# Loading the first two pairs with two neighbouring tokens per partition, and issuing the weights after the second and fourth batch

## The chip, the cores and the metric

The kernel runs on one NeuronCore of a Trainium2 chip. The metric is the device time of one execution in microseconds (us). Besides the timed runs there is one profiled execution, with a trace of every instruction. Five engines work side by side: TensorE (PE; its weight loads are shown as PEld), VectorE (DVE), ScalarE (ACT), GpSimd (POOL) and SyncE (SP), which issues transfers. Each engine executes its own instructions in the order in which they were written; semaphores make one engine wait for another.

## What is computed

A gated linear attention over four batches of eight heads, 768 tokens and a head dimension of 48, and after it a feed-forward layer over all 3072 tokens:

```
f = 1 / (1 + exp(-f_logit))
for t in range(S):
    state = f[:, :, t, :, None] * state + einsum('bhd,bhe->bhde', k[:, :, t], v[:, :, t])
    y[:, :, t] = einsum('bhd,bhde->bhe', q[:, :, t], state)
x = y as (batch * tokens, 384)
h = x @ w_in            # 384 -> 2048
g = maximum(0.01 * h, h)
out = g @ w_out         # 2048 -> 384
```

Inputs and outputs are float32 in the chip's main memory.

## The kernel before

The recurrence is cut into chunks of 128 tokens, six per batch. A *pair* j is one chunk of two batches, so there are twelve pairs, two for each chunk; pairs 0 and 1 hold the first chunk of batches 0, 1 and 2, 3. In the names below the first number is the pair, the second the batch of the pair (0 or 1; a 2 stands for both), the third a part. The steps of a pair are these:

- `Lf`, `Lk`, `Lq`, `Lv` (`load`, line 96): SP loads one input of one batch, 192 KB, with a token on each of 128 partitions. A partition gets eight separate runs of 192 bytes, one per head. `inp` has six buffers per input.
- `gate` (118) on ScalarE: exp and ln give the log of the gate, `lf`. The two instructions take 128x384 elements for one batch; from pair 4 on both batches at once.
- `cs` (124) on TensorE: a matmul with the upper triangle `ut` sums `lf` over the tokens, and four small ones with `ones_col` sum it over the whole chunk. `dec` (133) on ScalarE takes the exponentials of these.
- `k` and `q` (143, 149): k and q are scaled. `K_DVE` and `Q_DVE` say for how many pairs that is done on VectorE; after that it is done on POOL.
- `v` (155) on POOL: two casts of v, `v_b` and `v2`.
- `tk`, `tq` (170) transpose on TensorE, `ck`, `cq` (175) copy the result out on VectorE.
- `sc` (184): the scores q·k, 16 matmuls for both batches. `mk` (195): VectorE multiplies them with the triangle. `mx` (201): 32 matmuls of 32 columns each for two batches (56 where there is a state from earlier chunks), which give `py`; `xt` (229) copies that into `xT`.
- `pt`, `sf`, `sb` (233, 239, 244): the state of the chunk on TensorE, its addition on VectorE, its decay and cast on POOL.
- `up` (251): six matmuls with `w_in`, eight such groups in a pair; `pr` (260): the leaky relu on ScalarE; `dn` (264): four matmuls with `w_out`, eight such groups in a pair; `ob` (270) on VectorE and `st` (274) on SP: the copy and the store of 128 rows of the result.
- `WI` and `WO` (`weights`, 101): POOL copies one element of a loaded input into `gate_w`, and by that waits for this load; then it issues the transfers of `w_in` (nine) or `w_out` (four), which cast to bfloat16 on the way.

All of this is written in one long list of words, `order` (292 to 348), and emitted in that order; no scheduler moves anything. So an engine's order of work is the order of its words in the list: what is behind a waiting instruction on the same engine waits as well. The tag `g` of the PSUM has four buffers, used in turn by `cs`, `tp`, `pw`, `py` and `pt`; `pm` and `po` have two each.

Before the list come the constants (59 to 83): on VectorE the zeroing of the padding columns, on POOL `ut`, `ident`, `ones_col`, then `v2s` and the states.

In the list before, SP loads in the order f, f, k, q, v of pair 0 and then the rest in turn; `WI_1` stands behind `q_1_1` and waits for the second v load of pair 1, `WO_2` waits for that of pair 2. On POOL `v_0_0`, `v_0_1` and `v_1_0` stand ahead of `WI_1`, `v_1_1` behind it.

Of the kernel before, what the change touches and what calls it, by code (L numbers as in the profile page):

```python
# [9 lines left out]
FP32 = mybir.dt.float32  # L10
# [5 lines left out]
def kernel(  # L16
# [23 lines left out]
    BY_UNIT = 4  # L40
    K_DVE = 3
    Q_DVE = 2
# [31 lines left out]
    nc.gpsimd.memset(ones_col, 1.0)  # L74
    gate_w = const.tile([1, 8], FP32, tag="gate_w")
# [20 lines left out]
    def load(j, name, a):  # L96
        c, h = pairs[j]
        nc.sync.dma_start(out=raw(j, name)[:, a],  # L98
                          in_=srcs[name][2 * h + a, :, c * C:(c + 1) * C, :].rearrange("h t d -> t h d"))

    def weights(which, j):

        nc.gpsimd.tensor_copy(out=gate_w[:, 0:1], in_=raw(j, "v")[0:1, 1, H - 1, D - 1:D])
        if which == "in":
            for lo, hi in ((0, FF // 4), (FF // 4, FF // 2), (FF // 2, FF)):
                for kk in range(NK):
                    nc.gpsimd.dma_start(out=w_in_b[:, kk, lo:hi], in_=moe_w_in[kk * 128:(kk + 1) * 128, lo:hi])
        else:
            n = NF // 4
            for part in range(4):  # L110
                nc.gpsimd.dma_start(  # L111
                    out=w_out_b[:, part * n:(part + 1) * n, :],
                    in_=moe_w_out[part * n * 128:(part + 1) * n * 128, :].rearrange("(a p) n -> p a n", p=128))
# [3 lines left out]

    def gate(j, i):
        e = work.tile([128, 2, H, D], FP32, name="e_t", tag="e_t")
        a = half(j, i)  # L120
        nc.scalar.activation(e[:, a], raw(j, "f")[:, a], AF.Exp, scale=-1.0)  # L121
        nc.scalar.activation(lfs[j % NR][:, a, :, 0:D], e[:, a], AF.Ln, bias=1.0)  # L122

    def cs(j, a):
        lf = lfs[j % NR]
        t = st[j]["cs", a] = ps_g.tile([128, 512], FP32, name="cs", tag="g")
        nc.tensor.matmul(t[:, 0:H * D], ut, lf[:, a, :, 0:D], start=True, stop=True)  # L127
# [5 lines left out]
    def dec(j, a):  # L133
# [5 lines left out]
        if pairs[j][0] < NCH - 1:  # L139
# [3 lines left out]
    def scale_k(j, i):  # L143
        a = half(j, i)
        eng = nc.vector if j < K_DVE else nc.gpsimd
        eng.tensor_mul(khs[j % NR][:, a, :, 0:D], raw(j, "k")[:, a],  # L146
                       st[j]["em"][:, a].rearrange("t a (h d) -> t a h d", d=D))

    def scale_q(j, i):
        a = half(j, i)  # L150
        eng = nc.vector if j < Q_DVE else nc.gpsimd
        eng.tensor_mul(qhs[j % NR][:, a, :, 0:D], raw(j, "q")[:, a],  # L152
                       st[j]["a"][:, a].rearrange("t a (h d) -> t a h d", d=D))

    def cast_v(j, i):
# [3 lines left out]
        nc.gpsimd.tensor_copy(out=vb[:, a], in_=raw(j, "v")[:, a])  # L159
        nc.gpsimd.tensor_copy(out=v2[:, P2 * a.start:P2 * a.stop, 0:4:3, :],  # L160
                              in_=raw(j, "v")[:, a].rearrange("t a (p j) d -> t (a p) (j d)", j=2)[:, :, 32:64]
# [13 lines left out]
    def turn_out(j, a, x):  # L175
        nc.vector.tensor_copy(out=turned(j, x)[:, P2 * a:P2 * a + P2, :], in_=st[j].pop(("tp" + x, a)))  # L176
# [4 lines left out]
    def units(a):  # L181
        return range(2) if a == 2 else (a,)

    def score(j, a2):
        kT, qT = st[j]["kT"], st[j]["qT"]
        for a in units(a2):
            for i in range(2):
                st[j]["pw", a, i] = ps_g.tile([128, P2, 128], FP32, name="pw", tag="g")
            for p in range(P2):
# [5 lines left out]
    def mask(j, a, i):  # L195
        wm = st[j]["wm", a, i] = work.tile([128, P2, 128], BF16, name="wm", tag="wm", bufs=8)
        nc.vector.tensor_mul(wm, st[j].pop(("pw", a, i)), ut[:, None, :].to_broadcast([128, P2, 128]))  # L197
# [3 lines left out]
    def mix(j, a2):  # L201
# [10 lines left out]
        for a in units(a2):  # L212
# [16 lines left out]
    def x_out(j, a):  # L229
        xT = once(j, "xT", lambda: work.tile([128, NK, 2, 128], BF16, name="xT", tag="xT", bufs=3))  # L230
        nc.vector.tensor_copy(out=xT[:, :, a, :], in_=st[j].pop(("py", a))[:, 0:NK, :])  # L231

    def state(j, a):
        pt = st[j]["pt", a] = ps_g.tile([128, P2, 2 * D], FP32, name="pt", tag="g")
# [39 lines left out]
    def store(j, a):  # L274
# [13 lines left out]
        "WI": lambda j: weights("in", j), "WO": lambda j: weights("out", j),  # L288
# [4 lines left out]
    Lf_0_0 Lf_0_1 Lk_0_0 Lq_0_0 Lv_0_0 gate_0_0 Lf_1_0 gate_0_1 cs_0_0 Lk_0_1 dec_0_0 cs_0_1 Lq_0_1 dec_0_1 k_0_0  # L293
    Lv_0_1 v_0_0 q_0_0 tk_0_0 Lf_1_1 tq_0_0 ck_0_0 gate_1_0 pt_0_0 Lk_1_0 cq_0_0 sf_0_0 sc_0_0 Lq_1_0 cs_1_0 k_0_1
    q_0_1 Lv_1_0 tk_0_1 dec_1_0 v_0_1 mk_0_0_0 Lf_2_0 mk_0_0_1 tq_0_1 gate_1_1 Lk_1_1 ck_0_1 mx_0_0 cq_0_1 pt_0_1
    k_1_0 Lq_1_1 sb_0_0 sc_0_1 xt_0_0 Lv_1_1 mk_0_1_0 cs_1_1 v_1_0 mk_0_1_1 Lf_2_1 dec_1_1 sf_0_1 Lk_2_0 gate_2_0
    q_1_0 mx_0_1 tk_1_0 Lq_2_0 sb_0_1 xt_0_1 tq_1_0 pt_1_0 k_1_1 cs_2_0 Lv_2_0 dec_2_0 q_1_1 WI_1 ck_1_0 cq_1_0 tk_1_1
    gate_2_1 sf_1_0 tq_1_1 ck_1_1 sc_1_0 cq_1_1 cs_2_1 mk_1_0_0 dec_2_1 mk_1_0_1 sc_1_1 up_0_0 mk_1_1_0 v_1_1 mx_1_0
    mk_1_1_1 pr_0_0 up_0_1 Lf_3_0 sb_1_0 xt_1_0 mx_1_1 pr_0_1 pt_1_1 xt_1_1 up_0_2 sf_1_1 up_1_0 pr_0_2 k_2_0 sb_1_1
    pr_1_0 up_0_3 tk_2_0 pr_0_3 up_1_1 ck_2_0 pr_1_1 up_1_2 Lk_2_1 pr_1_2 up_1_3 Lq_2_1 up_0_4 q_2_0 pr_1_3 Lv_2_1  # L300
    pr_0_4 up_0_5 v_2_0 Lf_3_1 tq_2_0 pr_0_5 up_0_6 cq_2_0 gate_3_0 Lk_3_0 pt_2_0 up_1_4 sf_2_0 Lq_3_0 pr_0_6 cs_3_0
    k_2_1 q_2_1 pr_1_4 up_0_7 Lv_3_0 dec_3_0 tk_2_1 WO_2 tq_2_1 ck_2_1 up_1_5 cq_2_1 pr_0_7 sc_2_2 pr_1_5 up_1_6
    gate_3_1 mk_2_0_0 mk_2_0_1 up_1_7 pr_1_6 v_2_1 mk_2_1_0 cs_3_1 pr_1_7 mk_2_1_1 pt_2_1 dec_3_1 dn_0_0_0 sf_2_1
    mx_2_2 Lf_4_0 dn_1_0_0 xt_2_0 sb_2_0 xt_2_1 dn_0_0_1 sb_2_1 dn_1_0_1 up_2_0 k_3_0 pr_2_0 up_2_1 dn_0_0_2 pr_2_1
    dn_1_0_2 tk_3_0 up_2_2 Lk_3_1 ck_3_0 pr_2_2 up_2_3 Lq_3_1 dn_0_0_3 q_3_0 pr_2_3 Lv_3_1 dn_1_0_3 ob_0_0 v_3_0
    tq_3_0 Lf_4_1 ob_1_0 dn_0_1_0 cq_3_0 dn_1_1_0 st_0_0 dn_0_1_1 k_3_1 st_1_0 dn_1_1_1 q_3_1 dn_0_1_2 Lk_4_0 dn_1_1_2
    v_3_1 Lq_4_0 Lv_4_0 dn_0_1_3 gate_4_0 dn_1_1_3 ob_0_1 Lf_5_0 tk_3_1 ob_1_1 tq_3_1 up_2_4 st_0_1 ck_3_1 pt_3_0
    cq_3_1 pt_3_1 pr_2_4 up_2_5 st_1_1 sf_3_0 dn_2_0_0 sf_3_1 pr_2_5 Lk_4_1 up_2_6 Lq_4_1 sc_3_2 Lv_4_1 pr_2_6 up_2_7
    mk_3_0_0 Lf_5_1 dn_2_0_1 mk_3_0_1 pr_2_7 cs_4_0 Lk_5_0 mk_3_1_0 dn_2_0_2 dec_4_0 mk_3_1_1 cs_4_1 Lq_5_0 dn_2_0_3
    dec_4_1 mx_3_2 ob_2_0 Lv_5_0 v_4_0 dn_2_1_0 xt_3_0 st_2_0 xt_3_1 gate_5_0 dn_2_1_1 sb_3_0 Lf_6_0 up_3_0 Lk_5_1  # L310
    dn_2_1_2 sb_3_1 pr_3_0 Lq_5_1 up_3_1 k_4_0 dn_2_1_3 Lv_5_1 pr_3_1 up_3_2 ob_2_1 Lf_6_1 dn_3_0_0 pr_3_2 q_4_0
    tk_4_0 st_2_1 tk_4_1 ck_4_0 up_3_3 ck_4_1 Lk_6_0 pt_4_0 pt_4_1 pr_3_3 tq_4_0 sf_4_0 tq_4_1 up_3_4 Lq_6_0 cq_4_0
    v_5_0 Lv_6_0 dn_3_0_1 cq_4_1 pr_3_4 sf_4_1 up_3_5 gate_6_0 Lf_7_0 sc_4_2 up_3_6 Lk_6_1 mk_4_0_0 pr_3_5 mk_4_0_1
    Lq_6_1 cs_5_0 pr_3_6 up_3_7 mk_4_1_0 Lv_6_1 dec_5_0 dn_3_0_2 mk_4_1_1 cs_5_1 Lf_7_1 cs_6_0 pr_3_7 mx_4_2 dec_5_1
    Lk_7_0 dn_3_0_3 xt_4_0 sb_4_0 dec_6_0 Lq_7_0 cs_6_1 xt_4_1 dn_3_1_0 ob_3_0 sb_4_1 dec_6_1 Lv_7_0 up_4_0 dn_3_1_1
    st_3_0 pr_4_0 k_5_0 up_4_1 gate_7_0 Lf_8_0 dn_3_1_2 up_4_2 q_5_0 Lk_7_1 pr_4_1 dn_3_1_3 Lq_7_1 pr_4_2 tk_5_0
# [65 lines left out]
```

## Time and profile before

| | us |
|---|---|
| median of 3 runs | 198.18 |
| lowest and highest run | 196.0, 198.26 |
| the profiled execution | 197.44 |
| its span in the trace | 195.7 |
| TensorE busy | 177.3 (91%) |
| ScalarE, VectorE, POOL busy | 98.4, 93.4, 83.3 |
| bytes moved, mean rate | 27.08 MB, 138 GB/s |

The profiled execution is 1.74 us longer than its span; the median is 0.74 us above that execution. The profile's page gives the busy time of each engine, and the same in 40 slices of 4.9 us, a digit being tenths of a slice. The timeline shows start, duration, engine and line of instructions, and in brackets the idle time before them and what ended it. In a line of the table of stretches each engine has its busy time in that stretch, then come the granted TensorE clock, the mean share of the 16 DMA engines that was busy, and GB/s.

### The profile page before, as it was taken

To read this page: it belongs to the slowest core of one execution; us is meant where nothing else is said; L and a number is where in the kernel's file an instruction comes from. 1 tells how busy PE (TensorE), PEld (TensorE's weight loads), DVE (VectorE), ACT (ScalarE), POOL (GpSimd) and SP (SyncE) were. 2 spreads that over 40 slices of the span, in tenths; PEclk is the share of its full clock that TensorE was granted. 3 is DMA by queue.
4 is the path that set the end of the run, shared out by engine and by line. 5 is a ranking of instruction groups with operands and counts; after the bars stand their busy time and mean duration, and the time that the engine had idled before them with its cause. 6 is when DMAs were issued, how large, how long until landed. Compare 5 with 4: busy or idle time off the path is not lost.

```text
span 195.7 us, 5241 instructions
## 1 busy us (share of the span) xinstructions
PE 177.3 (91%) x2152; PEld 130.7 (67%) x2152; DVE 93.4 (48%) x203; ACT 98.4 (50%) x197; POOL 83.3 (43%) x145
## 2 busy tenths in 40 slices
PE   0686379999999999999979999999999999999993
PEld 0455237777667687787756867777777777777761
DVE  2699614273327438347581149168373146553111
ACT  5645415893234748776155752854324736154430
POOL 8145845928400762795332902984204420500000
PEclk9999999999999999999996999999999999999999
DMA  6999999899999999899999999220001110110112
GB/s 134 216 216 185 166 196 208 162 183 186 190 222 215 222 198 226 159 228 219 200 201 232 183 232 209 44 78 6 18 27 40 45 40 3 40 40 3 40 44 80
DMA packets 106728, 27.08 MB, mean 138 GB/s; under 512 B 100432, under 2 KB 106320, under 8 KB 106704
## 3 DMA queue, kind: packets, MB, share of 16 engines
q1 hardware_dynamic: 103296, 23.60, 57.1%
q0 software_dynamic: 3408, 3.15, 10.1%
q8 instruction: 17, 0.28, 0.6%
q14 instruction: 7, 0.06, 0.1%
HBM read 25.17 MB, written 4.72 MB: 153 GB/s over the span
## 4 chain that ended last, share of the span: by engine, by line
PE 69%; DMA 15%; SPq 11%; POOL 2%; issue 1%; ACT 1%; DVE 1%; POOLq 0%
PE po L267 30%; PE pm L256 25%; SPq L98 10%; DMA q_raw<-in_q_dram 7%; DMA w_out_b<-in_moe_w_out_dram 7%; PE py L225 4%; PE tp L173 4%; PE pw L192 2%; DMA f_raw<-in_f_logit_dram 1%; PE cs L127 1%; POOL w_out_b L111 1%; PE pt L236 1%; SPq L277 1%; POOL qh L152 0%; ACT e_t L121 0%
## 5 line engine op out<-in xcount | busy, mean ns | idle before, releaser
L262 ACT ACTIVATE gT<-pm 128x512 bf16<-128x512 f32 x96 | 57.0, 598 | 75.0 <-PE pm L256 74.5
L256 PE MATMUL pm<-xT,w_in_b 128*128 128x256 bf16 x576 | 79.7, 278 | 5.0 <-DMA w_in_b<-in_moe_w_in_dram 3.6
L267 PE MATMUL po<-w_out_b,gT 128*128 128x384 bf16 x384 | 75.9, 328 | 0.1
L256 PEld LDWEIGHTS <-w_in_b 128*128 128x128 bf16 x576 | 54.8, 99 | 19.1 <-DMA w_in_b<-in_moe_w_in_dram 4.4
L267 PEld LDWEIGHTS <-gT 128*128 128x128 bf16 x384 | 36.2, 98 | 17.2 <-issue 0.6
L197 DVE TENSOR_TENSOR wm<-pw,ut 128x512 bf16<-128x512 f32 x48 | 30.1, 683 | 9.1 <-PE pw L192 9.1
L272 DVE COPY osb<-po 128x384 f32<-128x384 f32 x24 | 13.4, 557 | 40.7 <-PE po L267 40.5
L246 POOL TENSOR_TENSOR sf<-sf,a_end 128x192 f32<-128x192 f32 x20 | 10.7, 535 | 27.1 <-DVE sf L242 26.4
L146 POOL TENSOR_TENSOR kh<-k_raw,em_t 128x768 bf16<-128x768 f32 (+1 forms) x10 | 15.0, 1495 | 15.0 <-ACT em_t L137 8.3
L249 POOL CAST sb<-sf 64x192 bf16<-64x192 f32 x40 | 14.2, 356 | 16.1 <-PE py L225 13.8
L159 POOL CAST v_b<-v_raw 128x384 bf16<-128x384 f32 (+1 forms) x16 | 10.9, 681 | 23.7 <-DMA v_raw<-in_v_dram 15.7
L231 DVE CAST xT<-py 128x384 bf16<-128x384 f32 x24 | 12.4, 553 | 15.7 <-PE py L225 15.2
L176 DVE COPY kT<-tp 128x512 bf16<-128x512 bf16 x24 | 9.8, 420 | 20.7 <-PE tp L173 20.7
L152 POOL TENSOR_TENSOR qh<-q_raw,a_t 128x768 bf16<-128x768 f32 (+1 forms) x12 | 16.8, 1399 | 0.5 <-DMA q_raw<-in_q_dram 0.4
L121 ACT ACTIVATE e_t<-f_raw 128x384 f32<-128x384 f32 (+1 forms) x16 | 11.0, 687 | 9.4 <-DMA f_raw<-in_f_logit_dram 9.3
L127 PE MATMUL cs<-lf,ut 128*128 128x384 bf16 x24 | 8.3, 366 | 7.3 <-ACT lf L122 6.6
L137 ACT ACTIVATE em_t<-cs 128x384 bf16<-128x384 f32 x24 | 11.8, 493 | 4.9 <-PE cs L130 4.6
L176 DVE COPY qT<-tp 128x512 bf16<-128x512 bf16 x24 | 9.8, 419 | 5.2 <-PE tp L173 5.0
L138 ACT ACTIVATE a_t<-cs 128x384 bf16<-128x384 f32 x24 | 12.0, 499 | 0.0
L122 ACT ACTIVATE lf<-e_t 128x384 bf16<-128x384 f32 (+1 forms) x16 | 10.9, 683 | 0.5
L173 PE MATMUL tp<-ident,kh 128*128 128x128 bf16 x96 | 9.6, 233 | 1.5 <-ACT a_end L141 1.0
L130 PEld LDWEIGHTS <-lf 128*128 128x128 bf16 x80 | 5.2, 103 | 8.1 <-issue 6.7
(40 smaller groups left out, 139.0 us busy)
## 6 DMA issues: line engine op xcount, KB each, us to landing
f_raw<-in_f_logit_dram SPq DMA_DIRECT2D x24, 192.0 KB, 3.7
k_raw<-in_k_dram SPq DMA_DIRECT2D x24, 192.0 KB, 3.7
q_raw<-in_q_dram SPq DMA_DIRECT2D x24, 192.0 KB, 3.8
v_raw<-in_v_dram SPq DMA_DIRECT2D x24, 192.0 KB, 3.8
out_dram<-osb SPq DMA_DIRECT2D x24, 192.0 KB, 2.0
w_out_b<-in_moe_w_out_dram POOLq DMA_DIRECT2D x4, 384.0 KB, 9.5
w_in_b<-in_moe_w_in_dram POOLq DMA_DIRECT2D x6, 128.0 KB, 6.1
w_in_b<-in_moe_w_in_dram POOLq DMA_DIRECT2D x3, 256.0 KB, 9.2
```

Source lines behind the costliest of these rows:

```text
L98: nc.sync.dma_start(out=raw(j, name)[:, a], in_=srcs[name][2 * h + a, :, c * C:(c + 1) * C, :].rearrange("h t d -> t h d"))
L146: eng.tensor_mul(khs[j % NR][:, a, :, 0:D], raw(j, "k")[:, a], st[j]["em"][:, a].rearrange("t a (h d) -> t a h d", d=D))
L152: eng.tensor_mul(qhs[j % NR][:, a, :, 0:D], raw(j, "q")[:, a], st[j]["a"][:, a].rearrange("t a (h d) -> t a h d", d=D))
L173: nc.tensor.transpose(tp[:, p, :], scaled(j, x)[:, a, 2 * p:2 * p + 2, :], ident)
L176: nc.vector.tensor_copy(out=turned(j, x)[:, P2 * a:P2 * a + P2, :], in_=st[j].pop(("tp" + x, a)))
L197: nc.vector.tensor_mul(wm, st[j].pop(("pw", a, i)), ut[:, None, :].to_broadcast([128, P2, 128]))
L231: nc.vector.tensor_copy(out=xT[:, :, a, :], in_=st[j].pop(("py", a))[:, 0:NK, :])
L249: nc.gpsimd.tensor_copy(out=sb[rows, a, :, i * D:i * D + D], in_=sf[rows, a])
L256: nc.tensor.matmul(pm[:, i, :], w_in_b[:, kk, ff * 128:(ff + 1) * 128], st[j]["xT"][:, kk].rearrange("t a s -> t (a s)"), start=(kk == 0), ...
L262: nc.scalar.activation(gT[:, 2 * g:2 * g + 2, :], st[j].pop(("pm", g)), AF.Prelu, alpha=0.01)
L267: nc.tensor.matmul(po, st[j]["g"][:, ff, 128 * a:128 * a + 128], w_out_b[:, ff, :], start=(ff == 0), stop=(ff == NF - 1))
L272: nc.vector.tensor_copy(out=osb, in_=st[j].pop(("po", a)))
```

## The change

The change touches the first two pairs (`DUO = 2`) and the order of everything up to pair 7; behind `st_7_0` the list is the same.

- For these two pairs a load puts the 128 tokens of batch a on partitions 64a to 64a+63, two neighbouring tokens on each partition. A partition then gets eight runs of 384 bytes. The number of loads and their bytes stay.
- The number that was the batch now is the *slot*: slot 0 holds the even tokens of both batches, slot 1 the odd ones. So `gate`, `k`, `q`, `v`, `tk`, `tq` of a slot need the loads of both batches.
- `cs` of a slot is two matmuls, with block triangles `ut2` and `st2`; the chunk's sums of both batches come in eight small matmuls with slot 1. `sc` of a slot is 16 matmuls of half the columns, `mk` multiplies with `mask0` or `mask1`, `mx` of the pair is 64 matmuls over 64 rows each, `pt` of the pair 16. `ck`, `cq` and `xt` write with other strides.
- POOL makes the new constants `ut2`, `st2`, `halves` and the masks: 29 more memsets and selects, ahead of those of `v2s` and the states.
- `weights` can wait for any load. `w_in` now follows the v load of batch 1 of pair 0 (the 8th load; before, the 17th), `w_out` that of pair 1 (the 16th; before, the 25th). On POOL the nine issues of `w_in` stand ahead of `v_0_0`, `v_0_1`, `q_1_0` and `q_1_1`; the four of `w_out` ahead of `v_1_0`, `v_1_1` and the first states.
- `Q_DVE` goes from 2 to 1: q of pair 1 is scaled on POOL.
- The list is new. On TensorE it begins with cs_0, transposes of pair 0, cs_1, scores of slot 0, and so on; `mx_0_2` stands behind `tq_1_0`, and `pt_1_2` behind `up_0_1`. The first group with `w_out`, `dn_0_0_0`, stands behind `up_0_4`. `st_0_0` stands between `Lv_2_1` and `Lf_3_1`.

```diff
+    DUO = 2
     K_DVE = 3
-    Q_DVE = 2
+    Q_DVE = 1
...
+    nc.gpsimd.memset(halves, 0.0)
+    for t, last in ((ut2, True), (st2, False)):
+        nc.gpsimd.memset(t, 0.0)
+        for a in range(2):
+            rows = slice(64 * a, 64 * a + 64)
+            make_upper_triangular(nc, t[rows, rows], val=1.0, diag=last)
...
+            make_upper_triangular(nc, m[rows, 0, :], val=1.0, diag=s == 0)
+            make_upper_triangular(nc, m[rows, 1, :], val=1.0, diag=True)
...
+        if j < DUO:
+            nc.sync.dma_start(out=raw(j, name)[64 * a:64 * a + 64].rearrange("p a h d -> p (a h d)")
+                              .rearrange("p (h x) -> p h x", x=2 * D),
+                              in_=srcs[name][2 * h + a, :, c * C:(c + 1) * C, :]
+                              .rearrange("h (p s) d -> p h (s d)", s=2))
+            return
...
+        if j < DUO:
+            for s in range(2):
+                nc.tensor.matmul(t[:, 0:H * D], st2 if s > a else ut2, lf[:, s, :, 0:D], start=s == 0, stop=s == 1)
+            if a == 1 and pairs[j][0] < NCH - 1:
+                for p in range(P2):
+                    for s in range(2):
+                        nc.tensor.matmul(t[:, H * D + 2 * p:H * D + 2 * p + 2], lf[:, s, 2 * p:2 * p + 2, :], halves,
+                                         start=s == 0, stop=s == 1)
+            return
...
+                        for b in range(2):
+                            rows = slice(64 * i, 64 * i + D)
+                            nc.tensor.matmul(st[j]["pw", a, i][64 * b:64 * b + 64, p, :],
+                                             kT[rows, P2 * b + p, 64 * a:64 * a + 64], qT[rows, P2 * b + p, :],
+                                             start=True, stop=True)
...
     order = """
-    Lf_0_0 Lf_0_1 Lk_0_0 Lq_0_0 Lv_0_0 gate_0_0 Lf_1_0 gate_0_1 cs_0_0 Lk_0_1 dec_0_0 cs_0_1 Lq_0_1 dec_0_1 k_0_0
...
+    Lf_0_0 Lf_0_1 Lk_0_0 Lk_0_1 Lq_0_0 Lq_0_1 gate_0_0 Lv_0_0 Lv_0_1 gate_0_1 Lf_1_0 Lf_1_1 cs_0_0 Lk_1_0 Lk_1_1
+    cs_0_1 dec_0_0 Lq_1_0 WIv_0_1 Lq_1_1 dec_0_1 k_0_0 Lv_1_0 q_0_0 tk_0_0 Lv_1_1 gate_1_0 k_0_1 tq_0_0 Lf_2_0 q_0_1
+    gate_1_1 tk_0_1 ck_0_0 tq_0_1 cq_0_0 cs_1_0 ck_0_1 Lf_2_1 cs_1_1 cq_0_1 v_0_0 dec_1_0 sc_0_0 v_0_1 dec_1_1 k_1_0
+    Lk_2_0 q_1_0 mk_0_0_0 tk_1_0 mk_0_0_1 sc_0_1 q_1_1 k_1_1 tq_1_0 WOv_1_1 mk_0_1_0 mk_0_1_1 ck_1_0 cq_1_0 mx_0_2
+    pt_0_2 xt_0_0 v_1_0 xt_0_1 tk_1_1 Lq_2_0 sf_0_0 v_1_1 tq_1_1 up_0_0 sf_0_1 sb_0_0 gate_2_0 up_0_1 ck_1_1 cq_1_1
+    pt_1_2 sb_0_1 pr_0_0 cs_2_0 sf_1_0 pr_0_1 up_0_2 sf_1_1 dec_2_0 sc_1_0 up_0_3 mk_1_0_0 pr_0_2 sc_1_1 mk_1_0_1
...
```

## The prediction

> **What bounds the kernel now.** I read the page first (busy shares, slices, the chain that ended last), then the table of stretches, the timeline of the first 40 us and around 100 us, and the DMA's answer for 10 to 19 us.
>
> ```profile
> span 195.7 us, 5241 instructions
> PE 177.3 (91%) x2152; PEld 130.7 (67%) x2152; DVE 93.4 (48%) x203; ACT 98.4 (50%) x197; POOL 83.3 (43%) x145
> PE   0686379999999999999979999999999999999993
> DMA  6999999899999999899999999220001110110112
> ...
> PE 69%; DMA 15%; SPq 11%; POOL 2%; issue 1%; ACT 1%; DVE 1%; POOLq 0%
> ```
> TensorE has no room from the 7th slice on. What it loses lies in the first 27 us and in one dip in the middle. DMA is full to 121 us. So the change can win only what it takes off the start and the dip.
>
> ```profile
> 3.43 0.52 ACT L121 ACTIVATE e_t<-f_raw 128x384 f32<-128x384 f32 x1 [1.41 <-DMA f_raw<-in_f_logit_dram]
> 3.89 0.78 POOL L83 MEMSET sf<- 128x384 f32 x2
> ...
> 17.46 0.56 DVE L152 TENSOR_TENSOR qh<-q_raw,a_t 128x384 bf16<-128x384 f32 x1 [0.19 <-DMA q_raw<-in_q_dram]
> 19.20 0.18 POOL L103 COPY gate_w<-v_raw 1x1 f32<-1x1 f32 x1 [1.73 <-DMA v_raw<-in_v_dram]
> ...
> 24.53 0.40 PE L256 MATMUL pm<-xT,w_in_b 128*128 128x256 bf16 x1 [2.47 <-DMA w_in_b<-in_moe_w_in_dram]
> 24.77 0.53 POOL L107 DMA_DIRECT2D w_in_b<-in_moe_w_in_dram  x1 [0.98 <-DMA w_in_b<-in_moe_w_in_dram]
> 25.27 3.80 SPq L98 DMA_DIRECT2D v_raw<-in_v_dram  x1
> 25.29 0.52 POOL L159 CAST v_b<-v_raw 128x384 bf16<-128x384 f32 x1
> ...
> 29.12 5.05 SPq L98 DMA_DIRECT2D f_raw<-in_f_logit_dram  x1
> 29.91 0.50 PE L236 MATMUL pt<-v_b,kh 128*128 128x96 bf16 x4
> ```
> Load 1 lands at 3.43 and load 16 at 17.46: 0.94 us a load. The first weights wait for load 17 (19.20), the first up-projection for them (24.53). While POOL issues the nine weight DMAs its casts wait (next one 25.29), and beside the weights a load takes 3.4 to 5.1 us of SP's queue. TensorE is dense from 27.5; at 30.4 it has done all matmuls of pairs 0 and 1 before their down-projections except six of the eight up-projections of pair 0 and all of pair 1, and cs_2. I compare there.
>
> ```profile
> 100.65 0.84 ACT L121 ACTIVATE e_t<-f_raw 128x768 f32<-128x768 f32 x1 [2.40 <-DMA f_raw<-in_f_logit_dram]
> 102.90 1.23 PE L256 MATMUL pm<-xT,w_in_b 128*128 128x256 bf16 x6 [1.19 <-ACT gT L262]
> ```
> The dip: gate_9_0 waits 2.40 us for f_9, the relus queue behind it on ScalarE, TensorE idles 1.5 us (18.47 of 20 busy, granted clock 0.91 over 100 to 120) and then runs some 1.7 us slower than steady (six up matmuls and four down matmuls 1.2 us over, 56 mixes 0.5): 3.2 us in all.
>
> **Part 1, the loads.** Sixteen loads keep their bytes and halve their packets, 192 to 384 B. No row shows 384 B from SP. The nearest:
>
> ```profile
> q1 hardware_dynamic: 9421, 1.78, 101.0%
> 128.00:129.00 1.00, 1.00 (x11) 0.71 (x9) 0.55 (x2) 0.97 (x2) 1.00 (x2) 1.00 0.54 197
> ```
> In 10 to 19 us a 192 B packet cost 1.01 x 9 x 16 / 9421 = 15.4 ns of an engine; the lone store at 128 us 0.54 x 16 / 128 = 67 ns for 1536 B. A line between gives 22.8 ns for 384 B against 30.8 for two: 0.94 x 0.74 = 0.70 us a load. The ends are 0.47 (cost by packet alone) and 0.94 (by bytes alone). I take 0.70: load n lands at 3.19 + 0.70(n-1).
>
> The Trainium skill, page "SBUF — State Buffer", section "Door 1: The DMA port swizzle (why `[64,N]` ≈ `[32,N]`)", speaks against it: partitions 0 to 63 reach 8 of the 16 ports, for about 218 GB/s. By it a load takes some 0.90 us (estimate from that page), nearly today's, and the time is close to rival 2's; no run here shows a 64-partition load.
>
> **Part 2, POOL before the weights.** Now POOL's setup ends at 4.67. The change puts 29 memsets and selects before it. The old ones follow each other every 0.26 us at 128 columns (memset 0.73, select 1.01, next 1.25, 1.52, 1.76) and every 0.035 at one column. For 64 columns I take 0.18 x 24, with two wide memsets and three small: 5.1 us, end 9.8 (ends 5.9 and 11.7). Load 8, for which the weights now wait, lands at 8.1, so POOL decides: gate copy at 9.8, against 19.20. Eight issues of 0.56, the ninth after the first landing (5.2 us, as 19.33 to 24.53): POOL is free at 16.0. Queued behind these issues are v_0_0 and v_0_1 (0.8 each, 17.5) and q_1_0, q_1_1 (Q_DVE is now 1, so POOL's 0.91 instead of VectorE's 0.56; 18.4 and 19.3). On TensorE tq_1_0 (0.6) stands ahead of mx_0_2, so that starts at 19.0. The rest of the chain is ready by then: gates at 9.5 and 10.6, cs_1, sc_0 and masks by 17.5.
>
> **Part 3, TensorE's own additions** for each of two pairs: two cs matmuls and four small ones, 16 scores of half width, 32 mixes and eight states, all short. Sixteen mixes take 0.6 us cold (27.42 to 28.03) and 32 take 0.68 warm, so 64 cost 1.4 to 2.4; I take 1.7. Sixteen states 1.3 cold (four: 0.50, pipelined), 1.0 warm. From 19.0: mx_0_2 20.7, pt_0_2 22.0, tk_1_1 and tq_1_1 23.1, up_0_0 and up_0_1 (0.66 each) 24.4. The weights are there: first landing 15.2.
>
> **Part 4, the second weights.** WOv_1_1 waits for load 16. The squeeze starts 2.65 us after the gate copy (SP's issue at 21.85 is the first long one): 12.45. Fourteen loads have landed; two remain, at 2.05 (half of 4.1, by packets) to 4.1 us (the mean of 3.38, 3.80 and 5.05): 16.6 to 20.6, middle 18.6, before POOL's 19.3. So gate and four issues of 0.76 end at 22.5 and v_1_0, v_1_1 at 24.2; pt_1_2, which TensorE cannot pass, runs 24.4 to 25.4. TensorE then lacks, against 30.4 before, cs_2 (two of 0.5), sc_1 (1.2; 16 full-width scores took 0.62 at 41.01) and mx_1 (1.3 warm): level at 28.9, **1.5 us gained**. At the late end, 20.6, it is 0.2.
>
> **Part 5, what follows.** WOv_1_1 is also moved ahead of pair 0's state work on POOL (sf, sb); its reader is mx_2, some 20 us later, so it costs nothing unless POOL falls that far behind. w_out comes after w_in, finishing by some 36 us; the order asks for its first quarter at 29 and its last at 38. Loads 17 to 22 of pairs 2 and 3 crawl meanwhile; k_2_0 lands near 31, is asked for at 37. SP's st_0_0 now stands before Lf_3_1 and holds it to 41; four loads in flight cover that. I cost these at nothing; without cover each microsecond is paid in full. The DMA line runs 16 x 0.24 + one store (0.6) = 4.4 us ahead at f_9_1, but the new order asks for gate_9_0 4.0 us of TensorE work sooner (dn_4_1_3, up_5_1, transposes and scores of pair 6 now follow it) and TensorE is 1.5 ahead. The dip stays: 0 (ends -3.2 and +1).
>
> Sum: 195.7 - 1.5 = 194.2 of span; the profiled execution had 197.44 for 195.7, so 195.9. The median is 0.74 above that execution: **196.7 us**. Its own range, 195 to 199.5, is the late load 16 and a dip of half or slightly more.
>
> The Trainium skill, page "DMA: Bandwidth & Descriptors", section "Why small descriptors are slow (HBM only)", counts bytes/32 + 3 cycles a packet: 15 cycles for 384 B against 18, so 0.78 us a load (estimate). Load 16 would then decide, and the sum be some 199.5; no run shows the cycles.
>
> **Rivals.** 1. The dip goes too. If a load costs 0.50, f_9_1 is issued 7.6 us sooner, at 90.2, lands at 93.0, and gate_9_0 is asked for at 92.7: 3.2 us more, 193.5. For it: DMA is the longest line to 100 us and sheds 16 half-loads. Against: the packet rows give 0.70, and the order moves the gate forward too. A shorter POOL setup (8.1) would add up to 1.7.
>
> 2. Slower: the weights starve pair 1. It decides from load 16 landing after 19.3. If bytes set the price (0.94), load 8 lands at 10.0 and only ten have landed at the squeeze. Load 14, for q_1_0 and through tq_1_0 for mx_0_2, comes at 19 to 25, load 16 at 23 to 27; at 25.1 its copies and issues end at 28.3, the casts at 30.0, pt_1_2 at 31.0, level at 34.5: 4.1 us lost, 202.3, less up to 0.5 of dip: 201.8 (200 to 204). For it: loads of 3.4 to 5.1 us beside weights. Against: halved packets, if packets cost.
>
> **Chances.** Forecast 0.45, rival 1 0.25, rival 2 0.30. Two per cent, about what a measurement can tell here, puts the limits at 194.2 and 202.1. Rival 1 lies beyond for four fifths (0.20); rival 2 beyond for under two thirds (0.18); the rest, 0.62, is within. Leaving out a tenth at each end the range is 192.5 to 202.5.
>
> **What would show it.** Load landings 0.70 apart; POOL's gate copy near 9.8 and first cast near 16; mx_0_2 at 19.0; pt_1_2 at 24.4; the ScalarE wait for f_9 still near 2 us. Wrong if landings keep 0.9 apart, if load 16 comes after 21, if POOL's issues are held longer for landings, or if TensorE idles between 29 and 60.

## The result

The changed kernel takes **203.06 us** (median of 4 runs, 202.52 to 203.21); the kernel before, timed beside it, 197.63 (196.0 to 198.26, 4 runs). The ratio is 1.028, 95% interval 1.021 to 1.035: slower. The forecast was 196.7 in a range of 192.5 to 202.5. Ratios here and below compare undisturbed executions of both kernels, so they can differ from the ratio of two medians, and in the last experiment they rest on three of seven runs.

### The profile page after: what moved, and what is told of

It is laid out like the page before. It is cut to its first block, busy times and chain, and to the rows that moved or that the text cites. A ratio compares the mean times of both kernels' runs of the same rounds, so it can differ in the third digit from the quotient of the medians.

```text
span 201.0 us, 5514 instructions
## 1 busy us (share of the span) xinstructions
PE 175.2 (87%) x2268; PEld 129.3 (64%) x2268; DVE 92.0 (46%) x201; ACT 97.2 (48%) x195; POOL 89.4 (44%) x176
## 4 chain that ended last, share of the span: by engine, by line
PE 59%; SPq 16%; DMA 15%; ACT 3%; POOL 2%; issue 2%; DVE 1%; ACTq 0%; POOLq 0%
PE pm L348 25%; PE po L359 23%; SPq L125 10%; DMA f_raw<-in_f_logit_dram 9%; DMA v_raw<-in_v_dram 7%; SPq L120 6%; PE tp L222 3%; PE py L302 3%; ACT e_t L155 2%; PE pw L255 2%; POOL w_out_b L138 1%; PE cs L170 1%; ACT lf L156 1%; PE pt L328 1%; SPq L369 1%
## 5 line engine op out<-in xcount | busy, mean ns | idle before, releaser
L359 PE MATMUL po<-w_out_b,gT 128*128 128x384 bf16 x384 | 77.2, 326 | 0.9 <-ACT gT L354 0.9
L359 PEld LDWEIGHTS <-gT 128*128 128x128 bf16 x384 | 35.5, 98 | 17.3 <-ACT gT L354 2.0
L364 DVE COPY osb<-po 128x384 f32<-128x384 f32 x24 | 13.3, 556 | 41.2 <-PE po L359 41.2
L261 DVE TENSOR_TENSOR wm<-pw,ut 128x512 bf16<-128x512 f32 x40 | 25.1, 684 | 10.9 <-PE pw L255 10.9
L155 ACT ACTIVATE e_t<-f_raw 128x384 f32<-128x384 f32 (+1 forms) x16 | 10.9, 684 | 28.9 <-DMA f_raw<-in_f_logit_dram 28.9
L201 POOL TENSOR_TENSOR qh<-q_raw,a_t 128x768 bf16<-128x768 f32 (+1 forms) x14 | 18.6, 1328 | 4.1 <-DMA q_raw<-in_q_dram 3.4
L338 POOL TENSOR_TENSOR sf<-sf,a_end 128x192 f32<-128x192 f32 x16 | 8.1, 506 | 21.1 <-DVE sf L334 20.4
L313 DVE CAST xT<-py 128x384 bf16<-128x384 f32 x20 | 10.2, 553 | 11.2 <-PE py L302 11.0
L230 DVE COPY kT<-tp 128x512 bf16<-128x512 bf16 x20 | 8.3, 420 | 14.3 <-PE tp L222 14.3
L222 PE MATMUL tp<-ident,qh 128*128 128x128 bf16 x96 | 9.6, 233 | 3.4 <-POOL qh L201 3.1
L222 PEld LDWEIGHTS <-qh 128*128 128x128 bf16 x96 | 7.2, 104 | 5.3 <-POOL qh L201 3.3
L163 PE MATMUL cs<-lf,ut 128*128 128x384 bf16 x6 | 2.6, 509 | 9.1 <-ACT lf L156 9.1
```

The costliest lines, as they stand in the source:

```text
L155: nc.scalar.activation(e[:, a], part(j, "f", a), AF.Exp, scale=-1.0)
L201: eng.tensor_mul(qhs[j % NR][:, a, :, 0:D], part(j, "q", a), st[j]["a"][:, a].rearrange("t a (h d) -> t a h d", d=D))
L222: nc.tensor.transpose(tp[:, p, :], scaled(j, x)[:, a, 2 * p:2 * p + 2, :], ident)
L261: nc.vector.tensor_mul(wm, st[j].pop(("pw", a, i)), m[:, None, :].to_broadcast([128, P2, 128]))
L359: nc.tensor.matmul(po, st[j]["g"][:, ff, 128 * a:128 * a + 128], w_out_b[:, ff, :], start=(ff == 0), stop=(ff == NF - 1))
L364: nc.vector.tensor_copy(out=osb, in_=st[j].pop(("po", a)))
```

## The profile after

From the page of the changed kernel: the span, busy TensorE, three of the lines of 40 slices, and the shares of the chain that ended last.

```profile
span 201.0 us, 5514 instructions
PE 175.2 (87%) x2268; PEld 129.3 (64%) x2268; DVE 92.0 (46%) x201; ACT 97.2 (48%) x195; POOL 89.4 (44%) x176
PE   0536628999999985999899999999999999999993
PEclk9999985999999999999999999999999999999999
DMA  5999999968989899999998999711011010110112
...
PE 59%; SPq 16%; DMA 15%; ACT 3%; POOL 2%; issue 2%; DVE 1%; ACTq 0%; POOLq 0%
```

The span grew by 5.3 us, and TensorE is busy 2.1 us less. In the 6th slice (25 to 30 us) TensorE is busy for two tenths, in the 7th the granted clock is half, and in the 9th DMA has a hole. In the chain SP's queue has gone from 11% to 16% and TensorE from 69% to 59%: more of the time is set by loads waiting to be issued.

The timeline of the changed kernel, 5 to 46 us: start, duration, engine, line, operation, and in brackets the idle time before it and what ended that.

```profile
5.19 0.52 ACT L155 ACTIVATE e_t<-f_raw 128x384 f32<-128x384 f32 x1 [3.18 <-DMA f_raw<-in_f_logit_dram]
...
10.30 0.77 POOL L104 MEMSET sf<- 128x384 f32 x2
...
13.12 0.52 ACT L155 ACTIVATE e_t<-f_raw 128x384 f32<-128x384 f32 x1 [3.54 <-DMA f_raw<-in_f_logit_dram]
14.79 7.96 SPq L125 DMA_DIRECT2D f_raw<-in_f_logit_dram  x1
...
26.10 0.18 POOL L130 COPY gate_w<-v_raw 1x1 f32<-1x1 f32 x1 [3.64 <-DMA v_raw<-in_v_dram]
26.57 3.06 POOL L138 DMA_DIRECT2D w_out_b<-in_moe_w_out_dram  x4 [0.29 <-issue]
...
30.23 0.26 PE L323 MATMUL pt<-v_b,kh 64*128 64x96 bf16 x2 [3.77 <-POOL v_b L208]
31.04 0.75 PE L323 MATMUL pt<-v_b,kh 64*128 64x96 bf16 x14 [0.55 <-POOL v_b L208]
...
35.82 0.83 PE L348 MATMUL pm<-xT,w_in_b 128*128 128x256 bf16 x6
...
45.50 0.36 SPq L369 DMA_DIRECT2D out_dram<-osb  x1
```

The gate of a slot needs both batches, so the first one waits for load 2 (5.19) and that of pair 1 for load 10 (13.12): (13.12 - 5.19)/8 = 0.99 us a load. At 14.79 the first long issue of SP begins. By then eleven loads have landed. Loads 12 and 13 still keep the pace (15.2, 16.2); loads 14, 15 and 16, issued at 10.84, 11.77 and 12.72, take 7.1, 9.2 and 13.3 us to land, so they come at 17.9, 21.0 and 26.0. The second weights wait for load 16 (26.10). Their four issues take 3.06 us, then come the casts, and TensorE stands for 3.77 us before `pt_1_2`, whose second part begins at 31.04.

The table of stretches of the changed kernel. Read the first number behind the comma (TensorE busy) and, third from the end, the granted clock.

```profile
25.00:30.00 5.00, 1.45 (x13) 1.12 (x11) 1.46 (x4) 1.75 (x4) 3.56 (x6) 0.86 1.00 166
30.00:35.00 5.00, 4.23 (x48) 2.68 (x48) 2.20 (x6) 1.80 (x5) 4.40 (x12) 0.50 1.29 199
...
60.00:80.00 20.00, 16.94 (x226) 12.65 (x226) 11.91 (x26) 10.73 (x22) 10.84 (x17) 1.00 1.06 194
...
100.00:120.00 20.00, 19.69 (x292) 14.82 (x290) 10.48 (x23) 11.61 (x25) 12.93 (x19) 1.00 1.08 197
```

In finer stretches the clock falls at 28.6, which is 2.1 us into TensorE's pause, and is full again from 35.4. In between a group of six up matmuls takes 1.44 us; at 35.82 it takes 0.83. The point that the kernel before reaches at 30.4 is reached at about 35.7: 5.3 us late, as much as the span grew. So the whole loss is made in the first 36 us. Later the dip at 100 to 120 is nearly gone (0.31 us idle instead of 1.53), and 3.06 us idle at 60 to 80 have come in its place.

## The experiments

The theories: **A**, the weights come too early, and the kernel would be quicker with them behind pair 1; **B**, weights starve whatever loads are still to come; **C**, the change's loads are dear because a load fills only 64 partitions. Each edit is made in the changed kernel unless it says otherwise. In the expectations, which are shown as they were recorded, the letters belong to the run they stand in.

**The loads in the old form.** The first 16 loads fill 128 partitions in runs of 192 B; all else is the changed kernel's, so the tokens of the first two pairs are mixed up.

```diff
     def load(j, name, a):
         c, h = pairs[j]
-        if j < DUO:
+        if False:
```

> The changed kernel with its first 16 loads as before: 128 partitions, 192 B runs (the values are mixed, so the output is not the reference's). Theory A, bytes set the price of a load: landings 0.94 apart instead of 0.99, load 16 some 1 us earlier than 26.1, time 201.5 to 203. Theory B, the 384 B packets do help and the loss is in the new order: landings slower than with the change, time 204 or more.

203.46 us, 1.031 (1.024 to 1.038): between the two expectations, and no better than the changed form. The gates of pairs 0 and 1 wait until 4.98 and 13.86, 1.11 us a load, slower than with the change, as theory B of this run had it; load 16 is there by 28.9. So the change's form brings about a tenth per load over the old one in the same order, although it has half the packets.

That load 16 comes 2.8 us later here and the time is the same has a reason in the clock. Of this run, the second part of `pt_1_2` and the same group of up matmuls as above:

```profile
33.86 0.47 PE L323 MATMUL pt<-v_b,kh 64*128 64x96 bf16 x14 [0.52 <-POOL v_b L208]
...
36.75 0.83 PE L348 MATMUL pm<-xT,w_in_b 128*128 128x256 bf16 x6
```

Between the two starts lie 2.89 us; in the changed kernel it is 35.82 - 31.04 = 4.78 for the same work. In the runs with half heads, every second partition and two queues, further down, it is 2.88 to 2.89, at full clock. So the half clock costs the changed kernel 1.9 us, which the old form does not pay.

**Eight wide loads.** Each load takes 256 tokens of one batch on all 128 partitions, 384 KB in runs of 384 B (other tokens in the first two pairs).

```diff
-            nc.sync.dma_start(out=raw(j, name)[64 * a:64 * a + 64]...,
-                              in_=srcs[name][2 * h + a, :, c * C:(c + 1) * C, :]...)
+            if a == 0:
+                nc.sync.dma_start(out=raw(j, name)...,
+                                  in_=srcs[name][2 * h, :, c * C:(c + 2) * C, :]...)
```

> The changed kernel with its first 16 loads made as 8 of 384 KB, 256 tokens of one batch on all 128 partitions in 384 B runs (same bytes, other tokens, so the output is not the reference's). Theory A, bytes: 1.9 us a load of 384 KB, time as with plain loads, 201 to 203. Theory C, the half of the partitions is what makes the change's loads slow: 1.4 us a load or less (0.70 for 192 KB), load 16's data before 17 us, time 197 to 199.

196.31 us, 0.997 (0.991 to 1.002): just below theory C's 197 to 199, and 6.7 us less than the change, from the loads alone. The gates wait until 4.69 and 10.71, 0.75 us for 192 KB; the second weights' gate is ready at 21.05 without a wait. It leaves two readings: all 128 partitions, or half as many loads of twice the size.

**The same bytes on 128 partitions.** Sixteen loads of 192 KB in runs of 384 B, as in the change, but each with four heads of 256 tokens of one batch.

```diff
+            heads = slice(4 * a, 4 * a + 4)
-            nc.sync.dma_start(out=raw(j, name)[64 * a:64 * a + 64]...,
-                              in_=srcs[name][2 * h + a, :, c * C:(c + 1) * C, :]...)
+            nc.sync.dma_start(out=raw(j, name)...[:, heads],
+                              in_=srcs[name][2 * h, heads, c * C:(c + 2) * C, :]...)
```

> The changed kernel, whose first 16 loads keep their number, their bytes (192 KB), their packets (384 B) and their place in the order, but fill all 128 partitions: each takes four heads of 256 tokens of one batch (so the first two pairs compute with other tokens than the reference's). Theory C, that 64 partitions at a time are what makes the change's loads dear: 0.75 us a load as with the eight wide ones, so the first gate of pair 1 waits until about 11.2 (13.1 in the changed kernel), no idle TensorE of over 1.5 us after 20, and 196 to 198.5 us. Rival, that the wide loads were quick because they were half as many and twice as large: 0.95 to 1.0 us a load, the gate at 13, and 202 to 204 us.

196.62 us, 0.996 (0.991 to 1.001). The gate of pair 1 waits until 11.27, as theory C had it, though a load costs 0.87 between the two gates, because the first gate is earlier as well (4.33). One point was missed: TensorE still idles 2.13 us at 55.9 and 1.62 at 74.9, behind waits for f. The size of a load is not what makes it dear.

**Every second partition.** Still 64 partitions a load, but the even or the odd ones instead of the lower or the upper half.

```diff
-            nc.sync.dma_start(out=raw(j, name)[64 * a:64 * a + 64]...
+            nc.sync.dma_start(out=raw(j, name)[a:128:2]...
```

> The changed kernel, whose loads of the first two pairs fill every second partition (batch 0 the even ones, batch 1 the odd ones) instead of the lower or the upper 64; number, bytes, packets and order stay (so the first two pairs compute with mixed tokens). If it is which half of the partitions a load writes that makes it dear: 250 GB/s and more between 6 and 12 us, the first gate of pair 1 at about 11.2, 196 to 199 us, as with all 128 partitions. If it is that a load has only 64 partitions: 205 GB/s, the gate at 13, 202 to 204 us.

198.33 us, 1.001 (0.997 to 1.006), the gate at 11.32: the first expectation. So it is not the number of partitions either, but that the 64 lie in one half. The table of stretches for 6 to 11 us, when all four load at full tilt (last: GB/s), first of the changed kernel, then of half heads, then of every second partition, then of the old form in the new order:

```profile
6.00:11.00 5.00, 3.48 (x26) 2.01 (x26) 2.27 (x5) 2.98 (x8) 4.50 (x17) 1.00 1.30 203
```

```profile
6.00:11.00 5.00, 3.46 (x27) 2.20 (x27) 3.21 (x8) 2.15 (x6) 4.50 (x16) 1.00 1.18 271
```

```profile
6.00:11.00 5.00, 3.79 (x28) 2.29 (x28) 2.88 (x7) 2.78 (x8) 4.50 (x17) 1.00 1.07 269
```

```profile
6.00:11.00 5.00, 3.56 (x27) 2.07 (x27) 2.33 (x6) 2.77 (x8) 4.50 (x17) 1.00 1.43 187
```

The engines' share is above 1 in all of them, so the times of packets overlap in it; only the last column tells. Packets of 384 B give 270 GB/s when a load reaches both halves, 203 when it lies in one.

**Two queues.** If a lower and an upper load are in flight together, do they fill both halves?

```diff
-            nc.sync.dma_start(out=raw(j, name)[64 * a:64 * a + 64]...
+            (nc.scalar if a else nc.sync).dma_start(out=raw(j, name)[64 * a:64 * a + 64]...
```

> The changed kernel, whose loads of the first two pairs for batch 1 (the upper 64 partitions) are issued by ScalarE, in the same places of the order, so that a lower and an upper load are in flight at once. Theory C (64 partitions at a time): the two halves together go at about 0.75 us a load from the moment both queues run; the first gate of pair 1 waits until 11 to 12, and the time is 196 to 200 us. If instead a 384 B packet into 64 partitions has its price whatever runs beside it: 0.95 to 1.0 a load, the gate at 13 or later, 202 to 205 us. The issues that stand behind a gate on ScalarE could cost up to 1 us at the beginning in either case.

199.33 us, 1.014 (1.006 to 1.021). The time is theory C's, but the mechanism is the rival's: the rate in 6 to 11 us is 209 GB/s, hardly more than 203, and the gate of pair 1 waits until 14.8, since ScalarE's issues stand behind its gates. So two queues don't make a pair of halves into a whole. The 3.7 us gained come from elsewhere. With two issuers all sixteen loads are issued by 11.72, ahead of the first transfer of `w_in` (12.83). The last of them, from the DMA's answer for 11.73 to 11.75 us (KB, then us from issue to landing):

```profile
v_raw<-in_v_dram ACTq DMA_DIRECT2D x1, 192.0 KB, 7.1
```

So load 16 lands at 18.8, at the same price, (18.8 - 5.25)/14 = 0.97 us a load, and no weights are ahead of it. The second part of `pt_1_2` then begins at 29.15 instead of 31.04, 1.9 us sooner, and the clock stays full, which is the other 1.9.

**The loads by themselves.** Not the reference's computation: phases of eight loads, each begun when the one before has landed, and zeros as output.

```diff
+    for c in range(2):
+        phase(plain, c)
+        phase(change, c)
+        phase(heads, c)
...
+    phase(plain, 2, True)
+    phase(change, 2, True)
+    phase(heads, 2, True)
```

> Not the reference's computation: no recurrence and no matmuls, only loads in phases of eight (1.57 MB), each phase begun when the one before has landed, and zeros as output. Phases, twice each: the old form (128 partitions, 192 B); the change's (64 alternating, 384 B); half heads (128 partitions, 384 B); all in the lower 64; every second partition; the change's with the upper half issued by ScalarE; four loads of 384 KB. Then the first three once more beside the nine transfers of the first weights. If halves set the price: the change's form 203 to 210 GB/s, half heads and wide 260 or more, lower 64 the same as alternating or worse, the old form 215. If something else in the kernel makes the difference (setup on GpSimd, the order of the loads), the change's form goes at 250 or more when alone. Beside the weights I expect the old form to lose most (by packets 1024 against 512 a load): 2.5 to 4 us a load, half heads 1.5 to 2.5, the change's in between.

The timeline of this kernel. In each phase VectorE reads f, k, q and v as they land; from the reading of f to that of v there are six loads. Below: the old form, the change's, every second partition.

```profile
5.63 0.17 DVE L74 COPY seen<-f_raw 128x2 f32<-128x2 f32 x1 [4.32 <-DMA f_raw<-in_f_logit_dram]
...
11.65 0.17 DVE L74 COPY seen<-v_raw 128x2 f32<-128x2 f32 x1 [1.65 <-DMA v_raw<-in_v_dram]
...
16.53 0.17 DVE L74 COPY seen<-f_raw 128x2 f32<-128x2 f32 x1 [4.58 <-DMA f_raw<-in_f_logit_dram]
...
22.24 0.17 DVE L74 COPY seen<-v_raw 128x2 f32<-128x2 f32 x1 [1.63 <-DMA v_raw<-in_v_dram]
...
55.42 0.17 DVE L74 COPY seen<-f_raw 128x2 f32<-128x2 f32 x1 [3.98 <-DMA f_raw<-in_f_logit_dram]
...
59.94 0.17 DVE L74 COPY seen<-v_raw 128x2 f32<-128x2 f32 x1 [1.14 <-DMA v_raw<-in_v_dram]
```

| form of the load | us per 192 KB, first and second time | eight loads, issue to landing |
|---|---|---|
| old: 128 partitions, 192 B | 1.00, 1.06 | 10.35, 10.48 |
| change: halves in turn, 384 B | 0.95, 0.98 | 10.36, 10.28 |
| half heads: 128 partitions, 384 B | 0.89, 0.82 | 8.82, 8.50 |
| every second partition, 384 B | 0.75, 0.73 | 8.58, 8.84 |
| change, two queues | 0.86, 0.86 | 9.60, 9.79 |
| wide: 384 KB, 384 B | 0.73, 0.73 | 8.30, 8.09 |

With nothing beside it, the change's form takes as long for eight loads as the old one, and its price is that of the kernel, as the first expectation said. The half heads were expected at 0.76 or less and the old form at 0.91; both came out dearer. The phase of all loads in the lower half tells nothing: its two loads of an input write to the same place, so the second waits for the first. Beside the nine transfers of `w_in` the eight loads take 19.26 (old), 18.92 (change) and 17.56 us (half heads), which is 8.8, 8.6 and 8.9 more than the means alone. My expectation that the old form would lose most was wrong: the weights take some 8.7 us of DMA time from whatever stands behind them, in any form.

**v ahead of the second weights.** `WOv_1_1` moved behind `v_1_1` on POOL.

```diff
-    ... WOv_1_1 ... v_1_0 ... v_1_1 ...
+    ... v_1_0 ... v_1_1 WOv_1_1 ...
```

> The changed kernel with the w_out issues behind v_1_1 on POOL. Theory A, pair 1's late loads hold everything: pt_1_2 starts some 2 us sooner (near 28), but gate_2_0 on ScalarE still ends at 29 to 30, so 1.5 to 3 us of the 5 come back: 200 to 201.5. Theory B, POOL's queue is the loss: all of it comes back, 198 or less.

201.73 us, 1.023 (1.014 to 1.031): 1.3 us back by the medians, though the interval overlaps that of the changed kernel, and far from theory B's 198. The cast comes at 25.86 instead of 29.67, but the wait for load 16 before it (3.62) stays, and 1.81 us of waiting for `w_out` at 34.7 are new. POOL's order is at most the lesser part of the loss.

**Both weights behind pair 1.** The old places of the weights, with the change's loads and slots.

```diff
-    ... WIv_0_1 ... WOv_1_1 ...
+    ... q_1_1 WIv_1_1 ... v_1_1 WOv_1_1 ...
```

> The changed kernel with both weights behind the last load of pair 1 (w_in behind q_1_1 on POOL, w_out behind v_1_1). Theory A: pair 1 lands by 20.5, TensorE starts its first up-projection near 26 but is not stopped after it; 198 to 200.5. Theory B: the wait for the weights comes back on top of the order's loss, 203 to 206.

205.19 us, 1.039 (1.030 to 1.048), slower still, as theory B had it. Load 16, with no weights ahead of it, is there by 19.5. In the profiled execution (208.0, the longest one) TensorE waits for `w_in` (1.22 us at 24.95, 2.75 at 28.09) and for `w_out` (3.07 at 39.59). Theory A falls: the change's early weights are worth having; what is behind them is the trouble.

**Early weights in the kernel before.** One word: `WI` moved behind `v_0_1`, waiting for the 9th load; the old loads and order.

```diff
-    ... Lv_2_0 dec_2_0 q_1_1 WI_1 ck_1_0 ...
+    ... v_0_1 WI_0 ...
```

> The kernel before with one word moved: the weights of the first layer follow the second v load of pair 0 instead of that of pair 1, and stand on POOL behind v_0_1; loads, tokens and slots are the old ones. Theory B, that the early weights starve pair 1's loads whatever their form: the loads 13 to 17 take 3 us or more each, the gate of pair 1's batch 1 or its q and k wait until 23 to 27, and the time is 199 to 204 us. Rival A, that with the old order the weights, being 5 us earlier, take away the 2.5 us wait of the first up-projection and the loads do no harm: 194.5 to 197 us.

200.97 us, 1.022 (1.013 to 1.031). From the timeline of this kernel:

```profile
27.42 0.56 DVE L146 TENSOR_TENSOR kh<-k_raw,em_t 128x384 bf16<-128x384 f32 x1 [10.27 <-DMA k_raw<-in_k_dram]
```

k of pair 1, batch 1 (the 15th load), keeps VectorE for 10.27 us; TensorE is busy 1.68 us of the ten from 20 to 30. Theory B holds without any of the change's loads or slots: with seven or eight loads of 0.9 to 1 us still to come, the early weights cost some 4 us.

**The dip.** In the kernel before, `gate_9_0` moved behind `pr_5_3`.

```diff
-    st_4_1 gate_9_0 mk_6_0_1 up_5_2 ... pr_5_3 ...
+    st_4_1 mk_6_0_1 up_5_2 ... pr_5_3 gate_9_0 ...
```

> The kernel before with one word moved: the gate of pair 9 stands behind pr_5_3 on ScalarE instead of ahead of pr_5_1. The prediction priced the dip at 100 to 120 us at 3.2 us. If that price holds, and the wait for the load (2.4 us) is covered by the relus that are now ahead of it: 194.5 to 196 us. Rival: the wait is only handed on (the relus behind the gate still queue, or the later gate holds cs_9 and what follows): 197 to 199 us.

195.76 us, 0.996 (0.992 to 1.001): inside the first expectation, but the interval holds 1, so it is no proof of a gain. The stretches of the kernel before, and then of this one, around the dip:

```profile
100.00:105.00 5.00, 3.47 (x31) 2.17 (x28) 2.57 (x7) 4.31 (x9) 1.27 (x3) 0.81 1.06 228
105.00:110.00 5.00, 5.00 (x88) 4.00 (x87) 1.02 (x2) 2.17 (x6) 3.65 (x7) 0.84 0.99 194
```

```profile
100.00:105.00 5.00, 4.67 (x98) 3.61 (x96) 3.80 (x9) 3.89 (x8) 1.59 (x5) 1.00 1.10 237
105.00:110.00 5.00, 5.00 (x49) 3.95 (x47) 0.57 (x2) 4.39 (x12) 4.73 (x6) 1.00 1.01 193
```

The idle time falls from 1.53 to 0.33 us, and the low clock behind it is gone with it. The span is 2.0 us shorter, although TensorE was busy 1.1 us less up to 35 us (20.7 against 21.8): about 3.1 for the dip in these two executions, as priced (3.2). The timed runs show less of it.

**Fewer loads behind the weights.** The kernel before with that gate moved, `w_in` after the 13th load (v of pair 1, batch 0), and f of pair 2 loaded behind pair 1: three loads of pair 1 are left.

```diff
-    ... Lv_1_0 ... Lf_2_0 ... Lv_1_1 ... v_1_0 ... WI_1 ...
+    ... Lv_1_0 ... Lv_1_1 Lf_2_0 ... v_1_0 WI_1 ...
```

> The kernel before, with the gate of pair 9 moved behind pr_5_3, and the weights of the first layer following the 13th load (v of pair 1, batch 0) instead of the 17th, with f of pair 2 loaded behind pair 1. Theory: of the two early starts, this one leaves only three loads of pair 1 to be squeezed, so the 2.5 us wait of the first up-projection goes and little comes in its place: 193 to 195 us, faster than both kernels. Rival, that any load behind the weights takes 3 to 4 us: q_1_1 lands at 24 or later, and the time is 196 to 199 us.

196.96 us, ratio 0.989 (0.984 to 0.994): in the rival's range, two us above the theory's. The 2.47 us wait for `w_in` is gone, TensorE is dense from 24.2 instead of 27.5, but then:

```profile
44.19 0.81 PE L267 MATMUL po<-w_out_b,gT 128*128 128x384 bf16 x4 [2.04 <-DMA w_out_b<-in_moe_w_out_dram]
47.28 1.46 PE L267 MATMUL po<-w_out_b,gT 128*128 128x384 bf16 x8 [0.63 <-DMA w_out_b<-in_moe_w_out_dram]
```

With another 0.21 at 53.14, 2.9 us of what was won at the start go into waits for the second weights. The rival's mechanism did not show: loads 14 to 16 are issued by 14.08, ahead of the weights at 16.01, and the last is there by 18.27.

**Both weights sooner.** The same, and `WO` behind `v_2_0`, waiting for the first v load of pair 2 instead of the second.

```diff
-    ... v_2_0 ... q_2_1 ... WO_2 ...
+    ... v_2_0 WO_2 ... q_2_1 ...
```

> The kernel of the run before this one (gate of pair 9 later, first weights after the 13th load, f of pair 2 behind pair 1), with the second weights also moved: they follow the first v load of pair 2 and stand on GpSimd ahead of q of pair 2, batch 1, some 3.5 us sooner. In the run before, TensorE was dense from 24.2 (27.5 in the kernel before) and then waited 2.9 us for w_out at 44 to 53. Theory: the wait was only handed on, and with w_out sooner it goes: no wait over 0.5 us for w_out, 192.5 to 195 us, faster than both kernels. Rival: w_out then squeezes the loads of pairs 2 and 3 and TensorE waits for these instead: 196 to 198 us.

195.93 us (192.66 to 199.8, 7 runs) beside 198.01; ratio 0.982 (0.972 to 0.993). Three runs took 192.7 to 194.0, the other four 195.9 to 199.8, where the runs of the kernel before lie as well (195.4 to 199.8), so how much this wins stays open. The waits for `w_out` are gone. The profiled execution was the longest one (199.8). In it the rival's wait is there:

```profile
45.64 0.48 PE L127 MATMUL cs<-lf,ut 128*128 128x384 bf16 x1 [4.37 <-ACT lf L122]
```

ScalarE's gate before it had waited 4.58 us for f of pair 3. Whether the three quick runs are free of that wait no profile shows.

## Why the prediction was wrong

**The step that failed is Part 1, the price of a load**, and through it Part 4's "load 16 at 16.6 to 20.6". I read 0.70 us from a line between packets of two sizes, one from loads and one from a store, both over 128 partitions, and so left out the half into which the change's loads go. For packets that reach both halves the line was not far off: at 384 B they cost 0.73 to 0.89 by themselves and 0.75 in the kernel with wide loads. In one half at a time they cost 0.99, more even than the 0.94 that I took for the dear end. Together with the later first landing, load 16 would have come at 13.1 + 6 x 0.965 = 18.9 without weights (it is there by 19.5 in the run with both weights behind pair 1), where 3.19 + 15 x 0.70 = 13.7 was forecast: 5.2 us. The squeeze added 26.1 - 18.9 = 7.2 where I had 18.6 - 13.7 = 4.9: five loads, not two, were still to land when it began, and three of them were slowed. That is another 2.3. The 7.5 us between 18.6 and 26.1 are these two.

The runs with quick loads bear this out. In the same order, wide loads, half heads and every second partition give 0.997, 0.996 and 1.001 of the kernel before. The forecast was 0.993, which lies inside two of the three intervals: with loads near the forecast's price the rest of the working gives nearly its time, though a gain is not shown.

From load 16 on the sum held, but partly by luck. It landed 6.8 us behind POOL's 19.3, and the level point came 6.8 us later than forecast (35.7 against 28.9). The forecast took 0.5 for a `cs` and 1.2 for `sc_1`, which at full clock took 0.34 and 0.84 (two groups of 0.42) in the run with plain loads; the half clock, which I had not foreseen, made that work slow again.

- **The rule on one half of the partitions** (the Trainium skill, page "SBUF — State Buffer", section "Door 1: The DMA port swizzle (why `[64,N]` ≈ `[32,N]`)") had the sign and nearly the size: the estimate from it was 0.90, the measured price 0.99. By that page's bits every second partition reaches all ports, and the trace agrees: the rate there is 269 GB/s instead of 203. The same page's "Can I just issue two DMAs to hit both halves?" gives 6% for two in flight; here it was 3% in the kernel (209 against 203), some 12% alone (0.86 against 0.965). I had weighed the rule against a row of the trace that could not speak to it.
- **Part 2**, POOL's setup: 11.07 (forecast 9.8, ends 5.9 and 11.7). The gate copy came at 11.13, the first cast at 19.05 (16.0 before `v_0_0`), as the ninth issue was held until 18.47, longer than the 5.2 us that I allowed for a landing. `mx_0_2` began at 22.2 instead of 19.0. All this was covered by load 16.
- **Part 3**, TensorE's additions: 64 mixes took 1.0 us, not 1.7, and 16 states 0.82.
- **Part 4**, the price of a load beside the weights: the three that were slowed came 1.7, 3.1 and 5.0 us apart, 3.3 in the mean, inside the 2.05 to 4.1 given. The squeeze began 3.66 us after the gate copy (14.79 against 11.13), not 2.65. The count of loads still to come was what failed here, and it follows from Part 1.
- **Part 5**: from the level point to the end the two kernels take equally long, as forecast, but not for the reason given. The dip did shrink (`gate_9_0` waits 1.50 us instead of 2.40); waits for f at 60 to 80 (`gate_6_0` 2.81 us, TensorE behind it 2.09) ate that up. Idle TensorE of 1.5 to 2.15 us behind a wait for f, between 55 and 85, is in every run that keeps the new order, with dear loads or quick ones, so it belongs to the order and not to the price of a load. `st_0_0`, which I had priced at nothing, leaves SP at 45.50, not 41, and DMA moves 49, 3 and 0 GB/s in the three us from 43 to 46. Whether those later waits come from it was not tested.
- **Not foreseen**: the half clock from 28.6 to 35.4 us, in and behind 3.77 us of idle TensorE. It cost 1.9 us (4.78 against 2.89). The Trainium skill, page "TensorE: Matmul & The Clock Gate", section "What's actually happening", gives half clock after an idle window of about 3.4 us. In this trace the clock had fallen 2.1 us into the pause, so it does not bear out that length, and the measurement decides.
- **Rival 2** had the mechanism, the place and nearly the time (201.8, 200 to 204). Its condition, a load of 0.94, is nearly what happened (0.99). It got 0.30 because the packet rows spoke against it; the loads alone show that halving the packets and halving the target cancel.

## What to carry to other kernels

Before pricing a transfer by its packets, look where it lands: find a row with the same partitions, or take the price that leaves out the gain. Weights that move ahead of loads cost these loads the weights' whole DMA time, so count what is still to be issued and to land when they start, and place them where few are left. A gain at the start is only kept if the next thing wanted (here `w_out`, then f of pair 3) comes sooner too.

## What the runs showed of the hardware

- Loads of 192 KB in runs of 384 B: 203 GB/s if loads fill the lower and the upper 64 partitions in turn, 269 on every second partition, 271 on 128.
- The old form made 211 GB/s in the old order at 6 to 11 us but 187 in the new order, and 192 alone with the batches in turn. What of the order or of the work beside it makes that difference stays open.
- The nine transfers of `w_in` add 8.6 to 8.9 us to eight loads of 192 KB issued beside them, whichever form the loads have.
- In the changed kernel the granted clock fell to half 2.1 us into a pause of TensorE of 3.77 us, and was half from 28.6 to 35.4; in the kernel before a pause of 1.19 us, ending at 102.90, was followed by half clock from 103.15 to about 106.5.
- From 25 to 31 us of the kernel before, the granted clock is shown as 1.00, although six up matmuls take 1.46 us at 27.97, against 0.82 at 37.08. Durations tell more than that column there.
